# Gated linear attention and a dropless mixture of experts: attention by half chunks on 64x64 tiles, with another order of the steps

## The chip, the core and the metric

The kernel runs on one core of a Trainium2 chip. Such a core has a matrix engine (TensorE, written PE in the profile, with its weight loads as PEld), a vector engine (VectorE, DVE), a scalar engine (ScalarE, ACT), a general engine (GpSimd, POOL) and a queue that issues transfers (SyncE, SP). Matmul results go to PSUM[...]; everything else lives in SBUF or in DRAM. The metric is the time of one execution on the device in microseconds, and the median of several executions is compared.

## What is computed

Gated linear attention over 4 batches, 8 heads, 768 positions and a head size of 48, and then a mixture of 8 experts in which each of the 3072 tokens goes to its one best expert. All data are float32.

```python
# attention, per batch and head
for t in range(S):
    state = alpha[t][:, None] * state + outer(k[t], v[t])
    y[t] = q[t] @ state
x = y as (B*S, H*D) rows                      # 3072 x 384

logits = x @ w_gate                           # 8 experts
expert_idx = argmax(logits); gate_w = softmax(logits)[expert_idx]
for e in range(E):                            # its own tokens only
    y[e's rows] = relu(x[e's rows] @ w1[e]) @ w2[e]      # 384 -> 1024 -> 384
out = gate_w * y
```

## The kernel before

**Attention.** The sequence is cut into 24 chunks of 128 positions (`C`; six per batch, `NB`), and heads are taken in pairs (`NP` = 4), the two heads of a pair at partitions 0 and 64 (`DP` = 64). Within a chunk the product of the gates is turned into a running sum of logarithms. For chunk s the steps are:

- `load` (L186): alpha, k, q and v from DRAM by SP's queue, 192 KB each.
- `logs` (L197): ln of alpha on ScalarE.
- `cums` (L207): one matmul with a triangular matrix gives the running sums in the bank `cum`; ScalarE writes their exponentials `icp` (negative) and `cp`.
- `decay_out`, `decay_in` (L216, L220): the last row of `cp`, the decay over the whole chunk, is stored to DRAM and read back as a column `E` per head pair, both by ScalarE's queue.
- `operands` (L230): GpSimd multiplies k by `icp` and q by `cp`, into `kqb`.
- `transposes` (L236): eight transposes on TensorE; ScalarE copies `kT`, VectorE copies `qT`.
- `scores` (L248): k times q for each head, eight matmuls of 128 columns; the two heads of a pair stand in two row halves of the array and write two banks, `sA` and `sB`. VectorE masks one side into `dA`; ScalarE copies the other and GpSimd masks it into `dB`.
- `attend` (L266): into the bank `y` first the product of the state `U` of the chunk before with q ("inter", L274), then v times the masked scores (L280); then the chunk's own key-value product `kvp` (L291). VectorE copies `y` to `yT`, and the next state is (`kvp` + `U`) times `E`, with the sum on VectorE (`acc`) and the product on GpSimd.
- `rows` (L308): `yT` times a fixed matrix `back` (which holds the gate's weights too) gives token rows and negative logits in the bank `xr`; VectorE sums the logits into `lgn`.
- `keep_rows` (L317): ScalarE copies the rows to `xs`, and SP stores them to `x_rows` in DRAM.

**Routing**, by groups of one to four chunks: `choose` (L325) finds each token's expert on VectorE, `rank_products` (L346) counts tokens by two small matmuls into free columns of the bank `kvp`, `slots_of` (L353) turns the counts into slots, `one_hots` (L369) writes them as one-hot rows, and `tokens_of_slots` (L377) multiplies these into a table of tokens by slot.

**Order.** Each engine does its instructions in the order in which the program writes them. The loop (L409) runs s from -5 to 24. In one iteration TensorE gets `cums(s+4)`, `transposes(s+2)`, `rows(s-1)`, `scores(s+1)`, then inter, values and key-values of `attend(s)`. So each step reads what another engine prepared an iteration ago. Loads are issued 5 (v) to 8 iterations ahead. In the last iteration the remaining routing is done, and `indices` (L384) gives the token list of every expert block.

**Experts.** GpSimd gathers the tokens' rows by index (`gather`, L495), `turn` (L518) transposes them, `layer1` and `layer2` (L536, L547) are the two products, and the results are scattered to the output. The weights stand in three buffers; `fetch1` and `fetch2` load them.

Two instructions of different engines on the same PSUM tile are ordered by semaphores that the framework adds.

## Time and profile before

| | us |
|---|---|
| median of 3 executions | 488.6 (488.29 to 490.05) |
| the profiled execution, its time | 489.74 |
| the profiled execution, first to last instruction (span) | 488.0 |
| attention: start to the last value matmul | 158 |
| seam: from there to the first transpose of the expert stage (170.25) | 12 |
| expert stage: 170.25 to the end | 318 |

| in one attention iteration, mean of one | ns |
|---|---|
| product on GpSimd (128x384) | 996 |
| copy of 128x512 from PSUM, VectorE / ScalarE | 687 / 593 |
| matmul record, 48 rows, 128 columns moved | 285 |
| matmul record, key-value, 48 columns moved | 222 |
| weight load record, 128 / 64 columns | 187 / 138 |

The profile lists a float32 matmul as two records, so eight products are 16. The records of matmuls that run together overlap, and a record is longer than the distance from one start to the next; the distance is what counts. Times in the lists are from the start of the span. An arrow gives the instruction that ended an engine's wait. "x16" means that 16 like instructions are merged in one line.

In slices of 12.2 us the sixteen transfer engines are busy all the time up to 120 us, at 160 to 210 GB/s[...]; 16 transfers of expert weights of 1536 KB stand later. TensorE's granted clock is full except at the seam, where the mean is 0.50 from 164 to 170 us and 0.52 from 170 to 178 us.

### The profile page before, as it was taken

To read this page: it belongs to the slowest core of one execution; us is meant where nothing else is said; L and a number is where in the kernel's file an instruction comes from. 1 tells how busy PE (TensorE), PEld (TensorE's weight loads), DVE (VectorE), ACT (ScalarE), POOL (GpSimd) and SP (SyncE) were. 2 spreads that over 40 slices of the span, in tenths; PEclk is the share of its full clock that TensorE was granted. 3 is DMA by queue.
4 is the path that set the end of the run, shared out by engine and by line. 5 is a ranking of instruction groups with operands and counts; after the bars stand their busy time and mean duration, and the time that the engine had idled before them with its cause. 6 is when DMAs were issued, how large, how long until landed. Compare 5 with 4: busy or idle time off the path is not lost.

```text
span 488.0 us, 7370 instructions
## 1 busy us (share of the span) xinstructions
PE 457.6 (94%) x2881; PEld 297.4 (61%) x2881; DVE 142.3 (29%) x391; ACT 103.2 (21%) x209; POOL 137.8 (28%) x226
## 2 busy tenths in 40 slices
PE   2999999999999389999999999999999999999992
PEld 0788888888898275555555555555555455555451
DVE  2344766665778421212401201101201201301100
ACT  3544544544421001101001111011111001101010
POOL 3556745555642270010124010016020020010020
PEclk9999999999999779999999999999999999999997
DMA  9999999889992151300726400537300040000000
GB/s 161 199 177 203 207 210 203 168 170 272 299 356 107 50 160 39 142 32 8 267 75 211 135 32 0 189 118 249 129 28 16 1 166 22 1 20 16 2 32 25
DMA packets 127213, 59.76 MB, mean 122 GB/s; under 512 B 110304, under 2 KB 121604, under 8 KB 127178
## 3 DMA queue, kind: packets, MB, share of 16 engines
q1 hardware_dynamic: 114818, 48.87, 39.6%
q0 software_dynamic: 3584, 10.34, 6.4%
q10 hardware_dynamic: 8776, 0.08, 1.0%
q8 instruction: 23, 0.38, 0.3%
q14 instruction: 12, 0.10, 0.1%
HBM read 49.70 MB, written 10.35 MB: 123 GB/s over the span
## 4 chain that ended last, share of the span: by engine, by line
issue 54%; PE 27%; POOL 11%; DVE 2%; DMA 2%; SPq 1%; ACT 0%; POOLq 0%; ACTq 0%
POOL out_dram L559 6%; POOL xg L499 5%; PE sA L254 5%; PE y L280 4%; PE tp L241 4%; PE xr L313 4%; PE cum L210 4%; PE y L274 4%; PE kvp L291 2%; SPq L194 1%; DMA a_sb<-in_alpha_dram 1%; DMA x_rows<-xs 1%; DVE yT L295 1%; DVE sc L330 0%; DVE dA L258 0%
## 5 line engine op out<-in xcount | busy, mean ns | idle before, releaser
L528 PE MATMUL hp<-xT,w 128*128 128x448 f32 (+2 forms) x402 | 148.4, 530 | 1.2 <-DVE xT L524 1.2
L553 PE MATMUL zp<-w,h_sb 128*128 128x384 f32 (+1 forms) x512 | 146.8, 488 | 0.0
L528 PEld LDWEIGHTS hp<-xT,w 128*128 128x128 f32 x402 | 77.4, 194 | 69.9 <-issue 65.0
L553 PEld LDWEIGHTS zp<-w,h_sb 128*128 128x128 f32 (+1 forms) x512 | 81.1, 177 | 62.4 <-issue 13.6
L559 POOL DMA_INDIRECT out_dram<-zo,g_idx x28 | 27.7, 988 | 251.7 <-ACT zo L558 251.7
L542 DVE TENSOR_SCALAR h_sb<-hp 128x448 f32<-128x448 f32 x32 | 20.0, 624 | 218.4 <-PE hp L528 218.4
L544 ACT ACTIVATE h_sb<-hp 128x448 f32<-128x448 f32 x32 | 17.4, 543 | 142.0 <-PE hp L528 142.0
L558 ACT ACTIVATE zo<-zp,gw 128x384 f32<-128x384 f32 x28 | 16.3, 581 | 133.6 <-PE zp L553 129.0
L210 PE MATMUL cum<-ln,cmask 128*128 128x384 f32 x48 | 24.7, 601 | 8.7 <-ACT cp L214 4.4
L499 POOL DMA_INDIRECT xg<-x_rows,g_idx x28 | 26.9, 960 | 12.2 <-issue 12.2
L241 PEld LDWEIGHTS tp<-ident,kqb 128*128 128x128 f32 x192 | 23.5, 146 | 7.9 <-issue 4.2
L254 PE MATMUL sA<-qT,kT 48*128 48x128 f32 x192 | 27.7, 285 | 0.0
L254 PE MATMUL sB<-qT,kT 48*128 48x128 f32 x192 | 27.7, 285 | 0.0
L233 POOL TENSOR_TENSOR kqb<-k_sb,icp 128x384 f32<-128x384 f32 x24 | 23.9, 996 | 8.8 <-ACT icp L213 8.6
L241 PE MATMUL tp<-ident,kqb 128*128 128x128 f32 x192 | 26.2, 282 | 0.0
L280 PE MATMUL y<-dA,vb 128*64 128x128 f32 x192 | 26.1, 279 | 0.0
L280 PE MATMUL y<-dB,vb 128*64 128x128 f32 x192 | 26.1, 279 | 0.0
L313 PE MATMUL xr<-back,yT 128*128 128x104 f32 x192 | 25.4, 275 | 0.7 <-DVE yT L295 0.5
L261 POOL TENSOR_SCALAR_AFFINE_SELECT dB<-dB 128x512 f32<-128x512 f32 x24 | 15.2, 634 | 37.3 <-ACT dB L260 23.8
L254 PEld LDWEIGHTS sA<-qT,kT 48*128 48x128 f32 x192 | 23.1, 187 | 2.6 <-issue 0.3
L313 PEld LDWEIGHTS xr<-back,yT 128*128 128x128 f32 x192 | 23.3, 192 | 1.5 <-issue 1.0
L234 POOL TENSOR_TENSOR kqb<-q_sb,cp 128x384 f32<-128x384 f32 x24 | 23.9, 996 | 0.0
(117 smaller groups left out, 403.0 us busy)
## 6 DMA issues: line engine op xcount, KB each, us to landing
w<-in_moe_w_dram SPq DMA_DIRECT2D x16, 1536.0 KB, 6.8
x_rows<-xs SPq DMA_DIRECT2D x24, 196.0 KB, 2.9
a_sb<-in_alpha_dram SPq DMA_DIRECT2D x24, 192.0 KB, 4.1
k_sb<-in_k_dram SPq DMA_DIRECT2D x24, 192.0 KB, 3.8
q_sb<-in_q_dram SPq DMA_DIRECT2D x24, 192.0 KB, 4.0
vb<-in_v_dram SPq DMA_DIRECT2D x24, 192.0 KB, 4.6
Eb<-decay_rows ACTq DMA_DIRECT2D x40, 0.8 KB, 3.0
xg<-x_rows,g_idx POOLq DMA_INDIRECT x28, 3.1
```

Source lines behind the costliest of these rows:

```text
L210: nc.tensor.matmul(cum[:], lhsT=cmask[:], rhs=d["ln"][:], start=True, stop=True)
L233: nc.gpsimd.tensor_tensor(kq[:, 0, :, :D], d["k"][:], heads(d["icp"]), op=ALU.mult)
L234: nc.gpsimd.tensor_tensor(kq[:, 1, :, :D], d["q"][:], heads(d["cp"]), op=ALU.mult)
L241: nc.tensor.transpose(tp[:, p, :], pair(kqb[s % 4][:, i], p), ident[:])
L254: nc.tensor.matmul(t[:, p, :], lhsT=d["kT"][r : r + D, p, :], rhs=d["qT"][r : r + D, p, :], start=True, stop=True,)
L280: nc.tensor.matmul(y[r : r + DP, p, :], lhsT=d["v"][:, 2 * p + i, :], rhs=d["d" + "AB"[i]][:, p, :], start=(c == 0 and p == 0), stop=True, ...
L313: nc.tensor.matmul(xr[:, p, :], lhsT=d["yT"][:, p, :], rhs=back[:, p, :], start=True, stop=True)
L499: nc.gpsimd.indirect_dma_start(out=xg[:, j, :], out_offset=None, in_=x_d[:, :], in_offset=bass.IndirectOffsetOnAxis(ap=i, axis=0),)
L528: nc.tensor.matmul(hp[:, c0:c1], lhsT=w1[:, a, f * C : (f + 1) * C], rhs=xT[:, a, c0:c1], start=(a == 0), stop=(a == DB - 1), skip_group_c ...
L542: nc.vector.tensor_relu(h[:, f, :cols], hp[:, :cols])
L553: nc.tensor.matmul(zp[i * m : (i + 1) * m, :], lhsT=h[:, f, c0 : c0 + m], rhs=w2[:, f, :], start=(f == 0), stop=(f == FB - 1), skip_group_ ...
L559: ins = nc.gpsimd.indirect_dma_start(out=out[:, :], out_offset=bass.IndirectOffsetOnAxis(ap=idx, axis=0), in_=zo[:], in_offset=None, bound ...
```

## The change

The change is in attention alone, with the places where weights are fetched.

**Half chunks.** `HALVES` numbers four combinations of a half j of the chunk (64 positions) and a head a of the pair. Scores are computed only within a half: 64 keys by 64 queries. The state is kept twice: `U[:, 0]` before the first half and `U[:, 1]` before the second, which is `U[:, 0]` plus the key-value product of the first half. Each of inter, scores, values and key-values becomes 16 matmuls of 64 by 64 (48 rows where the head size is summed), four to a head pair, each in another quarter of the array. `at(j, a)` puts the output of head a of half j in the partitions that make this so. Rows take `yT` of both halves, as two column tiles, with a `back` for each half.

**PSUM.** One tile `y` of two banks, one per half, holds both the values (`y_ps`) and the key-values (`kv_ps`). One tile `scp` of two banks, one per head, holds the scores and four columns for the decays (`last_ps`). The sums' bank has spare columns in which `rank_products` now write.

**Decays.** The way through DRAM goes. A matmul with the last column of the identity takes the last row of `cp` out as a column, eight per chunk, and ScalarE copies them to `E`.

**Order.** s runs from -4 to 23, and an iteration gives TensorE: decays(s+2), key-values(s+1) and values(s); sums(s+3), ranks of the last group and transposes(s+2); inter(s+1) and scores(s+2); rows(s). VectorE: `state(s+1)` (both sums), `qT`, slots, one product with the mask for both heads (`dAB`), `lgn`, `choose`, one-hots. ScalarE: `E`, `results(s)` (the copy `yT`), `icp`, `cp`, `kT`, `xs`, ln. GpSimd: the decay of the state, then the operands.

**Loads** are listed in order of need (`loads`), three to four iterations ahead, with five buffers each for alpha, k and q. The store of a chunk's rows is issued at the start of the next iteration, ahead of that iteration's loads. Expert 0's weights are asked for in iteration 17 and expert 1's in iteration 20; before it was iteration 15, and expert 1's stood after attention in the program.

```diff
+    HALVES = [(j, a) for j in range(2) for a in range(2)]
+    def at(j, a):
+        return DP * (a ^ j)
...
-        def decay_out(s):
-            if s % NB + 1 < NB:
-                nc.scalar.dma_start(e_d[s : s + 1, :], st[s]["cp"][C - 1 : C, :])
-        def decay_in(s):
...
+        def decays(s):
+            for p in range(NP if s < NT else 1):
                 for a in range(2):
+                    h = (2 * p + a) * D
+                    nc.tensor.matmul(
+                        last_ps[half(a), p : p + 1], lhsT=cpb[s % 3][DP:, h : h + DP], rhs=ident[DP:, C - 1 :],
+                        start=True, stop=True, skip_group_check=True,
                     )
+            if s < NT and s % NB + 1 < NB:
+                st[s]["E"] = Eb[s % len(Eb)]
+                nc.scalar.copy(st[s]["E"][:], last_ps)
...
+        scp = ps.tile([C, 2, 512], F32, name="scp")
+        sc_ps = scp[:, :, : NP * DP].rearrange("r b (p t) -> r b p t", p=NP)
+        last_ps = scp[:, 1, NP * DP : NP * DP + NP]
+        y = ps.tile([C, 2, 512], F32, name="y")
+        y_ps = y[:, :, : NP * DP].rearrange("r b (p t) -> r b p t", p=NP)
+        kv_ps = y[:, :, NP * DP : NP * (DP + D)].rearrange("r b (p d) -> r b p d", p=NP)
+
+        def inter(s):
+            d = st[s]
+            for p in range(NP):
+                for j, a in HALVES:
+                    if j or s % NB:
+                        nc.tensor.matmul(
+                            y_ps[at(j, a) : at(j, a) + DP, j, p, :],
+                            lhsT=Ub[s % 2][head(a), j, p, :], rhs=d["qT"][head(a), p, half(j)],
+                            start=(p == 0), stop=False, skip_group_check=True,
+                        )
...
         def scores(s):
             for p in range(NP):
+                for j, a in HALVES:
                     nc.tensor.matmul(
+                        sc_ps[half(j), a, p, :], lhsT=d["kT"][head(a), p, half(j)], rhs=d["qT"][head(a), p, half(j)],
+                        start=True, stop=True, skip_group_check=True,
                     )
+            d["dAB"] = work.tile([C, 2, NP, DP], F32, name="dAB", bufs=3)
+            nc.vector.tensor_tensor(
+                d["dAB"][:], sc_ps, m64[:, None, None, :].to_broadcast([C, 2, NP, DP]), op=ALU.mult,
             )
 
         def attend(s):
+            n = s + 1
+            for p in range(NP):
+                for j, a in HALVES:
+                    if n < NT and (j == 0 or n % NB + 1 < NB):
+                        nc.tensor.matmul(
+                            kv_ps[half(a), j, p, :],
+                            lhsT=kqb[n % 4][half(j), 0, 2 * p + a, :], rhs=st[n]["v"][half(j), 2 * p + a, :D],
+                            start=(p == 0 and (s < 0 or (j == 0 and s % NB == 0))), stop=True, skip_group_check=True,
+                        )
...
+                    nc.tensor.matmul(
+                        y_ps[at(j, a) : at(j, a) + DP, j, p, :],
+                        lhsT=d["v"][half(j), 2 * p + a, :], rhs=d["dAB"][half(j), a, p, :],
+                        start=False, stop=True, skip_group_check=True,
+                    )
...
+        def state(s):
             c = s % NB
+            U = Ub[s % 2]
+            if c == 0:
+                nc.vector.tensor_copy(U[:, 1, :, :D], kv_ps[:, 0, :, :])
+            else:
+                nc.vector.tensor_tensor(U[:, 1, :, :D], kv_ps[:, 0, :, :], U[:, 0, :, :D], op=ALU.add)
             if c + 1 < NB:
+                acc = st[s]["acc"] = work.tile([C, NP, D], F32, name="acc")
+                nc.vector.tensor_tensor(acc[:], kv_ps[:, 1, :, :], U[:, 1, :, :D], op=ALU.add)
+
+        def results(s):
+            st[s]["yT"] = work.tile([C, 2, NP, DP], F32, name="yT")
+            nc.scalar.copy(st[s]["yT"][:], y_ps)
...
+        def loads(s):
+            for n, i in (("v", s + 1 + AHEAD), ("k", s + 2 + AHEAD), ("q", s + 2 + AHEAD), ("a", s + 3 + AHEAD)):
+                if 0 <= i < NT:
+                    load(n, i)
...
+        for s in range(-4, NT):
+            last = s == NT - 1
+            do(store_rows, s - 1)
+            loads(s)
+            if 0 <= s + 2 <= NT:
+                decays(s + 2)
+            if s + 1 >= 0:
+                attend(s)
+            do(state, s + 1)
+            if 0 <= s + 1 < NT and (s + 1) % NB + 1 < NB:
+                decay(s + 1)
+            do(results, s)
+            do(cums, s + 3)
             do(operands, s + 3)
+            ranked = []
+            for g in groups_of:
+                if g[-1] == s - 1:
+                    if last:
+                        sums_tile()
+                    ranked.append(rank_products(g, st["sums"][:, Dm : Dm + len(g) * E]))
             do(transposes, s + 2)
+            for r in ranked:
+                slots_of(*r)
+            do(inter, s + 1)
+            if s == NT - 2:
+                seen = work.tile([C, 2, 1], F32, name="seen")
+                nc.vector.tensor_copy(seen[:], y_ps[:, :, NP - 1, :1])
+            do(scores, s + 2)
+            if last:
                 while hots:
                     one_hots(hots.pop(0))
+                route = ps.tile([C, NP, C], F32, name="tp", bufs=2)[:].rearrange("r p t -> r (p t)")
+                tokens_of_slots(0, NT - 4)
+            do(rows, s)
+            do(keep_rows, s)
+            for g in groups_of:
+                if g[-1] == s:
+                    choose(g)
+            for _ in range(min(len(hots), 2 if len(hots) > 2 else 1)):
                 one_hots(hots.pop(0))
+            do(logs, s + 4)
+            late_consts(s + 2)
+            if s in (NT - 7, NT - 4):
+                e = (s - NT + 7) // 3
+                w_t[e] = fetch1(e), fetch2(e)
+        store_rows(NT - 1)
```

## The prediction

> **What bounds the kernel now.** I read the page first: what is busy, and when.

> ```profile
> span 488.0 us, 7370 instructions
> PE 457.6 (94%) x2881; PEld 297.4 (61%) x2881; DVE 142.3 (29%) x391; ACT 103.2 (21%) x209; POOL 137.8 (28%) x226
> ...
> PE   2999999999999389999999999999999999999992
> ...
> DMA  9999999889992151300726400537300040000000
> ```

> Each of the 40 slices is 12.2 us. TensorE is full except in the first slice and in slices 14 and 15, the seam between attention and the expert stage. The expert stage begins with the first transpose at 170.25 us (timeline) and keeps TensorE busy to the end; its work is not edited. So the question is when attention ends. Second, the timeline of one attention iteration on TensorE; columns are start and duration in us, then the instruction.

> ```profile
> 83.86 0.62 PE L291 MATMUL kvp<-vb,kqb 128*64 128x48 f32 x16
> ...
> 84.41 0.91 PE L210 MATMUL cum<-ln,cmask 128*128 128x384 f32 x2
> ...
> 85.16 1.04 PE L241 MATMUL tp<-ident,kqb 128*128 128x128 f32 x8
> ...
> 86.03 1.04 PE L313 MATMUL xr<-back,yT 128*128 128x104 f32 x8
> ...
> 88.09 1.09 PE L274 MATMUL y<-qT,Ub 48*64 48x128 f32 x16
> ```

> Each start is the end of the stage before. Sums 0.75, transposes 0.87, rows 0.97, scores 1.09 (87.00 to 88.09), inter 1.02 (to 89.11), weighted values 1.02 (to 90.13), key-value 0.55: 6.27, the chain of waits gives 6.16 after its rounding of ends. There is no hole: transposed tiles are used one iteration later, so no copy is waited for. Chunks that begin a batch lack inter; the mean from rows(0) (24.84) to inter(23), which follows rows(22) at 155.59, is 5.9.

> Third, the copies beside it:

> ```profile
> 84.68 0.35 DVE L301 TENSOR_TENSOR acc<-kvp,Ub 128x192 f32<-128x192 f32 x1
> ...
> 85.42 0.49 ACT L213 ACTIVATE icp<-cum 128x384 f32<-128x384 f32 x1 [0.58 <-PE cum L210]
> ...
> 85.81 0.49 ACT L214 ACTIVATE cp<-cum 128x384 f32<-128x384 f32 x1
> ...
> 86.18 0.59 ACT L246 COPY kT<-tp 128x512 f32<-128x512 f32 x1
> ```

> Read the steps between starts: 0.39 and 0.37, so ScalarE takes 1.35 from the start of icp to the end of kT. Fourth, a wait in the tail that decides much below:

> ```profile
> 158.62 1.12 PE L313 MATMUL xr<-back,yT 128*128 128x104 f32 x8
> ...
> 161.12 0.18 DVE L315 TENSOR_REDUCE lgn<-xr 128x8 f32<-128x32 f32 x1
> ...
> 161.47 0.48 ACT L320 COPY xs<-xr 128x384 f32<-128x384 f32 x1 [4.44 <-DVE lgn L315]
> ```

> ScalarE was idle for 4.44 us, the rows were done at 159.74, yet it waited for a VectorE read of other columns of the same PSUM tile. Accesses of two engines to one PSUM tile are kept apart, reads too.

> [...]scores to inter, the next start comes 0.21 after the last instead of 0.11 and the second 0.16 after that, 0.15 in all. [...](y from dA and dB load 6 to 7 ns apart and run together); no run here shows four tiles.[...]

> **The change part by part.**

> 1. TensorE's own work. With 64 columns of weights, a key-value pair takes (0.62 - 0.222) / 7 = 0.057: eight pairs take 0.62 with the last one's tail. A quad of four 64x64 tiles streams 64 or 48 columns; I take one quad pass as one such pair, 0.058. Bounds: 0.055 and 0.116 (two pairs in turn). Key-value, values, inter and scores are 8 quad passes each: 4 x 0.47. The new decays are 16 loads with one column on one row half: 8 pairs, 0.47. Rows on two column tiles: 104 columns against the old bound of 128 weight columns; the first old rows pass, its weights ready, took 0.09; 8 x 0.09 = 0.73. Sums 0.75 and transposes 0.87 stay. Sum 4.70; four mode changes at 0.15 add 0.6 (the old order had about as much): 5.3, against 6.2. If this were all, 0.9 x 22 iterations = 20 us would go.

> 2. The new order makes TensorE wait. Time 0 is the first decay matmul; decays, key-value and values end at 1.41, the last one's tail at 1.63. state (VectorE) reads the key-value columns of the two banks that the values are written to; by the bank wait it starts after both: U 1.68 to 2.03, acc 2.06 to 2.41 (0.35 each). results (ScalarE) reads the same banks: from 2.58 (0.17 handover, as 161.30 to 161.47) to 3.17. Behind it in ScalarE's order stand icp 3.07, cp 3.46, kT 3.83 to 4.42. And scores now need kT of their own iteration: 4.57 (0.15 handover, as ScalarE's ln to the first sums, 4.15 to 4.30). TensorE could have been there at 3.8: transposes end at 3.13, and only inter (0.47, with its mode change) lies between. Scores to 5.05, rows to 6.0, next decays at 6.15. dA's product (0.69) ends at 6.02 and lets the decays, which share a scores bank, start at 6.17. So an iteration takes about 6.15: the 0.9 saved is waited away.

> 3. rank_products now write the sums' bank and stand between sums and transposes. By the bank wait they start after cp: 4.1 to 4.3 in such an iteration (choose, 1.64 on VectorE in 147.03 to 148.67, delays state by 0.3), so transposes start at 4.35, not 2.26. kT and qT then follow, scores at 6.3, not 4.57, and the period is about 8.0: +1.85 each. In-loop groups with sums: after chunks 3, 7, 11, 15 and 18, so 5 x 1.85 = 9.2 us. Bounds 0 (no wait) and 12 us. In the old order the ranks went to the key-value bank, and no reader stood before them.

> 4. Decays without DRAM: 40 loads and 20 stores leave ScalarE's queue (1.0% of 16 engines x 488 = 4.9 us of DMA time). Not on the path: 4.8 us of DMA per chunk (alpha loads issued from 39.76 to 78.19: 8 chunks) hides under an iteration of either length. The select on POOL (0.63) and the copies dB and dA of one side go; they were no bound. The new copy of E (128x4, ScalarE) falls ahead of results, while ScalarE waits anyway. Cost 0.

> 5. Loads in order of need. Iteration 0 now needs the 12th load, alpha of chunk 3, instead of the 14th. The 12th was issued at 11.20 and lands some 4 us later; logs 0.52: 15.8 at the earliest. The sums at 4.30 took 1.62 where 0.91 is normal[...] and the pipeline is a chain of short waits, so I take 17.5 for the start of iteration 0 and 23.6 for the end of rows(0), against 25.7 (24.84 + 0.87). Gain 2, bounds 0 and 4.

> 6. Stores move ahead of the loads in SP's order, and wait for xs(s-1), so five loads stand behind each such wait; they have three iterations of lead, 18 us against 4. Cost 0; if the lead went, 1 us an iteration. Expert 1's weights are now asked for in iteration 20, and hidden until after 170 us. Both 0. So are the tiles that move from one pool to another, the copy to `seen` and the lone decay pair of chunk 24: each is one short instruction where its engine is free.

> 7. Tail. After rows(22), rank(22) waits for choose(22), then 20 token matmuls (16 took 1.52, so 0.085 apart), then rows(23): 2.3 + 0.1 + 1.7 + 0.9 and 0.3 to lgn(23), 5.3. Before: 155.59 to 161.12, 5.5. The rest is the same. 0, bounds -1 and +2 (the clock's slow stretch of 13.7 us there may shift).

> Sum: rows(0) to rows(22). After: 19 iterations at 6.11 (the batch's last chunk saves 0.24) = 116.1, ranks 9.2, then 6.1, 6.1 and 4.6 for iterations 20 to 22, which lose sums, transposes and scores in turn but wait for choose: 142.1. Before: 155.6 - 25.7 = 129.9. So +12.2, less 2 from the start: +10.2. The profiled execution took 489.74 (span 488.0 and 1.7 around it): 499.9. The median is 488.6: 498.8, rounded to 499.

> **The rivals.**

> A. The case above: the chain through VectorE and ScalarE sets the period, and ranks wait. 499; with the period 0.3 shorter or longer, 492 to 506.

> B. On the other side, faster: state starts after its own key-value matmuls, results do not wait for it, ranks do not wait for cp. Then qT is the last: transposes end 3.29, copy to 4.02, scores 4.17, period 5.7: 19 x 5.66 + 5.7 + 5.7 + 4.5 = 123.4, against 129.9: -6.5 - 2 = 480. It decides if the bank wait is not applied between disjoint columns here; the row reduction and xs speak against it.

> C. The chain holds but ranks do not stall: 499 - 9 = 490.

> D. Four tiles do not run together: pairs, so +0.47 for key-value, values and scores: 1.41 x 21 = 30: 529. For it: only diagonal pairs are seen. Against: column pairs and row pairs each run at full overlap.

> E. Issue-bound quads: eight instructions in 58 ns at the 6.5 ns seen within pairs leave no room; 0.073 a quad gives about 0.48 x 21 = 10: 509.

> **How the numbers follow.** A 0.50, B 0.19, C 0.13, D 0.10, E 0.08. A is the likeliest: 499. 481 to 512 leaves out D and about half of B. What can be told from no change is 0.5%, 2.4 us: 486.2 to 491.0. Slower: A, D, E and little of C, 0.69. Same: most of C and edges, 0.13. Faster: B, 0.18. A's own range is 492 to 506.

> **What would show it.** Step 1: 16 or 32 matmuls a group and quads 0.058 apart in the timeline. Step 2: results released by DVE acc, and scores' weight loads idle some 0.7 us released by ACT kT; a period of 6.1 between sums. Step 3: rank matmuls released by ACT cp, five iterations near 8. Step 5: rows(0) ending near 23.6. I am wrong if TensorE shows no hole ahead of scores, or if rows(22) ends before 155.

## The result, and the profile after

| | before | after |
|---|---|---|
| median, us | 488.5 | 509.0 |
| executions, us | 488.29 to 490.05 | 505.18 to 509.41 |
| ratio, 95% interval | | 1.039 (1.032 to 1.045) |
| the profiled execution: time / span, us | 489.74 / 488.0 | 505.18 / 503.3 |
| end of rows(0), us | 25.7 | 26.9 |
| end of rows(22), us | 155.6 | 172.4 |
| first transpose of the expert stage, us | 170.25 | 185.46 |
| from there to the end, us | 317.8 | 317.9 |

The kernel is 20 us slower by the medians, 15.3 by the two profiled spans. The expert stage is as long as before, so all of the 15.3 lies before it. Medians, here and below, are over all executions of a version; one that was disturbed (516.33 in after) is left out of the range and of the ratio. The profiled execution was the fastest: two others took 508.5 and 509.4, with a mean granted clock of 0.960, where the profiled one had 0.966.

The page of after first; the rows with digits are 40 slices of 12.6 us.

```profile
span 503.3 us, 11568 instructions
PE 453.3 (90%) x4997; PEld 288.3 (57%) x4997; DVE 128.7 (26%) x396; ACT 104.3 (21%) x229; POOL 127.0 (25%) x206
...
PE   4898988888878839999999999999999999999992
...
PEclk9899999999899578999999999999999999999997
...
q8 instruction: 40, 0.66, 0.6%
```

And two rows of the page of before that were not shown:

```profile
PEclk9999999999999779999999999999999999999997
...
q8 instruction: 23, 0.38, 0.3%
```

TensorE's row in attention was all nines and is eights now: it is busy for 4 us less in all and yet the span is longer, so it waits. Two more things differ. The granted clock dips within attention (slices 2, 11 and 14), not only at the seam. And queue 8, which brings pieces of the program itself, moved 40 packets of 16 KB where it was 23. TensorE's instructions, matmuls and weight loads together, are 9994 against 5762.

The timeline of one iteration of after, with the columns start, duration, instruction; what stands in brackets is the idle time before it and what ended that:

```profile
93.22 0.91 PE L225 MATMUL cum<-ln,cmask 128*128 128x384 f32 x2
...
93.80 0.36 DVE L344 TENSOR_TENSOR acc<-y,Ub 128x192 f32<-128x192 f32 x1
...
94.27 0.59 ACT L348 COPY yT<-y 128x512 f32<-128x512 f32 x1 [1.25 <-DVE acc L344]
...
94.75 0.50 ACT L228 ACTIVATE icp<-cum 128x384 f32<-128x384 f32 x1
...
95.14 0.50 ACT L229 ACTIVATE cpb<-cum 128x384 f32<-128x384 f32 x1
...
95.50 0.61 ACT L267 COPY kT<-tp 128x512 f32<-128x512 f32 x1
96.16 0.56 PEld L298 LDWEIGHTS scp<-qT,kT 48*64 48x64 f32 x32 [0.69 <-ACT kT L267]
96.17 0.69 PE L298 MATMUL scp<-qT,kT 48*64 48x64 f32 x32 [0.55 <-ACT kT L267]
...
96.79 0.93 PE L356 MATMUL xr<-back,yT 128*64 128x104 f32 x16
...
99.29 0.91 PE L225 MATMUL cum<-ln,cmask 128*128 128x384 f32 x2
101.79 0.19 PE L397 MATMUL cum<-ohs,ones_sq 128*128 128x32 f16 x1 [1.59 <-ACT cpb L229]
```

This is the chain of step 2. VectorE's `acc` ends at 94.16, ScalarE's copy of the results follows at 94.27, then `icp`, `cp` and `kT` one behind the other, and scores start when `kT` is done; TensorE's weight loads were idle for 0.69 us. From sums to sums it is 6.07. The last line is the next iteration, in which the ranks wait 1.59 for `cp`: step 3.

What no step had is in the timeline of TensorE alone, in after:

```profile
40.12 0.23 PE L323 MATMUL y<-dAB,vb 64*64 64x64 f32 x1
41.12 0.68 PE L323 MATMUL y<-dAB,vb 64*64 64x64 f32 x27 [0.77 <-issue]
41.73 0.91 PE L225 MATMUL cum<-ln,cmask 128*128 128x384 f32 x2
...
163.22 0.34 PE L298 MATMUL scp<-qT,kT 48*64 48x64 f32 x7
164.63 0.58 PE L298 MATMUL scp<-qT,kT 48*64 48x64 f32 x25 [1.07 <-issue]
165.14 1.37 PE L356 MATMUL xr<-back,yT 128*64 128x104 f32 x16
```

(The two parts are from two stretches of that timeline.) TensorE stops for about a microsecond in the middle of a group of like matmuls, whose operands are all there, and the profile names nothing that it waited for. I call that a hole, and count each step of more than 0.42 us between two starts on TensorE that no wait explains, less the usual 0.06 (the two records of the sums always start 0.43 apart; there a hole counts when it adds more than 0.42 to that). After has six in attention, 5.1 us in all (at 36.4, 40.1, 80.3, 124.7, 143.2 and 163.3); before has none. In the records of queue 8, each of the six ends 1.3 to 1.6 us after a 16 KB piece of program has landed.

The holes also stand at fixed places of the program. Count all instructions of TensorE in the trace, control instructions too: 1217, 1473, 3521, 5825, 6593 and 7617 of them come before the ends of the six holes. Each of these numbers is 193 more than a multiple of 256. It is so for all 80 holes of all the runs here, and each of the 80 ends 1.2 to 1.7 us after a landing. So a hole is a wait at the edge of a piece of 256 instructions: TensorE has used up the piece it has, and the next one has only just landed.

In the last line of the view rows need 1.37 us where 0.93 is normal: from 165.48 on the granted clock is 0.5, for 10.24 us.

### The profile page after: what moved, and what is told of

The parts are those of the page before. It is cut to its first block, busy times and chain, and to the rows that moved or that the text cites. A ratio compares the mean times of both kernels' runs of the same rounds, so it can differ in the third digit from the quotient of the medians.

```text
span 503.3 us, 11568 instructions
## 1 busy us (share of the span) xinstructions
PE 453.3 (90%) x4997; PEld 288.3 (57%) x4997; DVE 128.7 (26%) x396; ACT 104.3 (21%) x229; POOL 127.0 (25%) x206
## 4 chain that ended last, share of the span: by engine, by line
issue 55%; PE 20%; POOL 9%; DVE 6%; ACT 5%; DMA 2%; SPq 0%; POOLq 0%; ACTq 0%; DVEq 0%
POOL out_dram L628 5%; PE xr L356 4%; PE scp L298 3%; POOL xg L568 3%; PE tp L262 2%; PE y L313 2%; PE y L323 2%; ACT icp L228 2%; PE scp L243 1%; ACT cpb L229 1%; ACT kT L267 1%; PE cum L225 1%; PE hp L597 1%; DVE Ub L341 1%; DMA a_sb<-in_alpha_dram 1%
## 5 line engine op out<-in xcount | busy, mean ns | idle before, releaser
L568 POOL DMA_INDIRECT xg<-x_rows,g_idx x28 | 26.9, 960 | 11.2 <-issue 7.9
L262 PEld LDWEIGHTS tp<-ident,kqb 128*128 128x128 f32 x192 | 24.3, 151 | 7.0 <-issue 4.7
L262 PE MATMUL tp<-ident,kqb 128*128 128x128 f32 x192 | 27.8, 292 | 0.0
L298 PE MATMUL scp<-qT,kT 48*64 48x64 f32 x768 | 17.6, 227 | 11.0 <-ACT kT L267 7.2
L265 DVE COPY qT<-tp 128x512 f32<-128x512 f32 x24 | 16.6, 691 | 34.9 <-PE tp L262 34.9
L255 POOL TENSOR_TENSOR kqb<-q_sb,cpb 128x384 f32<-128x384 f32 x24 | 24.0, 998 | 0.0
L356 PE MATMUL xr<-back,yT 128*64 128x104 f32 x384 | 23.7, 268 | 0.0
L366 ACT COPY xs<-xr 128x384 f32<-128x384 f32 x24 | 11.5, 478 | 58.0 <-DVE lgn L361 49.9
L323 PE MATMUL y<-dAB,vb 64*64 64x64 f32 x768 | 21.3, 230 | 2.3 <-issue 2.3
L303 DVE TENSOR_TENSOR dAB<-scp,m 128x512 f32<-128x512 f32 x24 | 16.6, 691 | 24.5 <-PE scp L298 24.1
L298 PEld LDWEIGHTS scp<-qT,kT 48*64 48x64 f32 x768 | 14.3, 137 | 14.2 <-ACT kT L267 9.5
L593 DVE COPY xT<-xtp 128x384 f32<-128x384 f32 (+1 forms) x32 | 14.8, 503 | 26.7 <-PE xtp L591 26.7
```

The source lines that it names most:

```text
L255: nc.gpsimd.tensor_tensor(kq[:, 1, :, :D], d["q"][:], heads(d["cp"]), op=ALU.mult)
L262: nc.tensor.transpose(tp[:, p, :], pair(kqb[s % 4][:, i], p), ident[:])
L298: nc.tensor.matmul(sc_ps[half(j), a, p, :], lhsT=d["kT"][head(a), p, half(j)], rhs=d["qT"][head(a), p, half(j)], start=True, stop=True, sk ...
L323: nc.tensor.matmul(y_ps[at(j, a) : at(j, a) + DP, j, p, :], lhsT=d["v"][half(j), 2 * p + a, :], rhs=d["dAB"][half(j), a, p, :], start=Fals ...
L356: nc.tensor.matmul(xr[half(j), p, :], lhsT=d["yT"][:, j, p, :], rhs=back[:, j, p, :], start=True, stop=True, skip_group_check=True,)
L568: nc.gpsimd.indirect_dma_start(out=xg[:, j, :], out_offset=None, in_=x_d[:, :], in_offset=bass.IndirectOffsetOnAxis(ap=i, axis=0),)
```

## The experiments

All are edits of after, but the last. Ratios are to the kernel before, run on the same chip (488.9 in the first group of four, 490.7 in the second, 490.6 in the third), so versions of different groups are compared by their ratios. The base period is the distance of two sums in an iteration with neither ranks nor a hole; half clock is the time between 18.7 us and the expert stage in which the granted clock was 0.5. Both and the holes are from the profiled execution.

| run | median | ratio (95%) | base period | holes: number, us | half clock |
|---|---|---|---|---|---|
| after | 509.0 | 1.039 (1.032 to 1.045) | 6.1 | 6, 5.1 | 16.6 |
| e1 results first | 520.3 | 1.063 (1.060 to 1.066) | 5.7 | 12, 20.2 | 36.6 |
| e2 ranks late | 501.8 | 1.021 (1.018 to 1.025) | 6.1 | 6, 6.4 | 20.5 |
| e3 scores with slack | 498.4 | 1.022 (1.017 to 1.028) | 5.4 | 6, 5.4 | 24.4 |
| e4 decays by DRAM | 512.8 | 1.045 (1.042 to 1.048) | uneven | 5, 3.7 | 24.3 |
| e5 ranks late and slack | 495.6 | 1.010 (1.006 to 1.014) | 5.4 | 14, 12.2 | 17.2 |
| e6 no inter | 515.0 | 1.046 (1.042 to 1.051) | 6.1 | 4, 4.7 | 32.9 |
| e7 old load order | 514.0 | 1.045 (1.041 to 1.049) | 6.1 | 5, 4.9 | 17.5 |
| e8 e5, decays by SP | 525.3 | 1.070 (1.066 to 1.073) | uneven | 3, 2.2 | 46.9 |
| e9 short filler | 519.8 | 1.059 (1.057 to 1.061) | 6.1 | 10, 9.8 | 31.0 |
| e10 long filler | 512.8 | 1.044 (1.037 to 1.051) | 6.1 | 6, 6.7 | 21.6 |
| e11 e5, wide decays | 498.9 | 1.012 (1.004 to 1.019) | 5.9 | 3, 3.0 | 15.8 |
| e12 before, store first | 490.5 | 1.000 (0.999 to 1.001) | 6.2 | 0, 0.0 | 4.6 |

Executions of one version of after lie up to 1.5% apart, so a difference of 3 us between two versions settles nothing. Holes and half clock are those of one traced execution each.

**e1: the results' copy ahead of the state.** It takes one link out of the chain.

```diff
+            do(results, s)
             do(state, s + 1)
...
-            do(results, s)
```

> Edit of the changed kernel: the copy of the results (ScalarE) is written ahead of the state's two sums (VectorE), which read the same two PSUM banks. Chain theory (VectorE sums, then the copy, icp, cp, kT, one behind the other because of the bank wait, set the period of 6.05 us): the copy starts 0.8 us earlier, kT ends about 0.4 earlier, qT is then last at 4.17 us from the first decay matmul instead of 4.5, so the period falls to 5.75 and the time by about 7 us, to 502. Rival (TensorE's own pace with four small tiles sets the period): no change, 509 within 2.

The chain was right: where nothing disturbed it the period fell from 6.07 to 5.70. But the whole got 11 us slower (ratio 1.063 against 1.039), with four times the time in holes and twice the half clock. The bank wait also stands the other way round now (timeline of e1):

```profile
64.69 0.59 ACT L348 COPY yT<-y 128x512 f32<-128x512 f32 x1 [2.02 <-PE y L323]
65.38 0.36 DVE L341 TENSOR_TENSOR Ub<-y,Ub 128x192 f32<-128x192 f32 x1 [3.43 <-ACT yT L348]
```

VectorE reads the key-value columns 0.1 us after ScalarE has read the value columns: two readers of one tile keep apart, whichever comes first. A faster chain alone gained nothing here, since holes and half clock grew.

**e2: ranks behind scores.**

```diff
-                    ranked.append(rank_products(g, st["sums"][:, Dm : Dm + len(g) * E]))
             do(transposes, s + 2)
-            for r in ranked:
-                slots_of(*r)
...
             do(scores, s + 2)
+                    ranked.append(rank_products(g, st["sums"][:, Dm : Dm + len(g) * E]))
+            for r in ranked:
+                slots_of(*r)
```

> Edit of the changed kernel: rank_products and slots_of stand after the scores instead of between sums and transposes. Rank theory (they wait for cp, which reads the same bank): five iterations of about 7.5 us become 6.1, so 7 us less, 502. Rival (those iterations are long because VectorE is busy with choose and slots): no change or 1 us less.

Four of the five rank iterations now take 6.2 to 6.3 us once the holes in two of them are taken off, against 7.1 to 8.2 in after; the fifth lies at half clock. The base period stayed at 6.1. Measured by the ratios (1.039 and 1.021), 8 us went. That agrees with the 8.1 us that the rank iterations of after take over its base period (step 3 below).

**e3: scores one iteration later.** `kT` then has a whole iteration.

```diff
-            do(scores, s + 2)
+            do(scores, s + 1)
```

> Edit of the changed kernel: an iteration computes scores(s+1) instead of scores(s+2), so kT and qT were copied an iteration ago, as in the kernel before. Chain theory: no wait ahead of scores, the period falls from 6.05 to TensorE's own 5.3 to 5.4, about 14 us less, 495; the ranks' waits stay. Rival (TensorE's own pace): no change. If instruction supply is a limit of its own, the gain is smaller, 5 to 9 us, with holes inside groups of like matmuls.

The base period fell to 5.4, so the wait for `kT` is worth 0.7 an iteration; the rank iterations at full clock still took 7.3. The start gained too: rows(0) end 2.6 us earlier, near the 23.6 of the prediction. Against that stand 7.8 us more of half clock, which at half speed is an estimated 3.9 us of work lost.

**e5: both.**

```diff
-                    ranked.append(rank_products(g, st["sums"][:, Dm : Dm + len(g) * E]))
...
-            do(scores, s + 2)
+            do(scores, s + 1)
+                    ranked.append(rank_products(g, st["sums"][:, Dm : Dm + len(g) * E]))
```

> Both edits of the changed kernel together: ranks after the scores, and scores(s+1) in place of scores(s+2). Chain theory alone: both waits go, 5.4 us an iteration throughout, 485. With the limit on TensorE's instruction supply (holes of 0.5 to 2 us, each ending 1.3 to 1.6 us after a 16 KB piece of its program has landed, 5 us in all in the changed kernel) more iterations meet it the faster they go: 490 to 498.

From e5's timeline:

```profile
69.06 0.69 PE L288 MATMUL y<-qT,Ub 48*64 48x64 f32 x32
...
69.57 0.65 PE L298 MATMUL scp<-qT,kT 48*64 48x64 f32 x32
69.66 0.60 ACT L267 COPY kT<-tp 128x512 f32<-128x512 f32 x1
...
70.15 0.19 PE L397 MATMUL cum<-ohs,ones_sq 128*128 128x32 f16 x1
```

Scores start before this iteration's `kT` is copied, and neither they nor the ranks wait. It has the lowest median of the versions with the change in it (e11's interval overlaps its own), and is still 1% slower than before. The holes more than doubled, to 14 and 12.2 us. The two waits were worth some 21 us (0.7 in each of 19 iterations, and 8); 7 of these came back as holes. TensorE now wants its 340 instructions every 5.4 us and not every 6.1.

**e6: no inter.** This leaves out the product of state and query, so the output lacks what earlier halves add. The values' first matmul then starts the sum in `y`, as inter's did.

```diff
-                        start=False, stop=True, skip_group_check=True,
+                        start=(p == 0), stop=True, skip_group_check=True,
...
-            do(inter, s + 1)
```

> Edit of the changed kernel that leaves out the product of the state with q (inter), so the output lacks what earlier positions add; 64 of TensorE's 340 instructions an iteration go, all of them from the place where it waits for kT anyway. Chain theory: the usual period stays 6.05 us. Supply theory: the holes inside groups go, 5 us, and the half-clock stretches of attention with them, 2 to 5 us: 500. Rival (TensorE's own pace): 0.6 us an iteration, 13 us less, with a period of 5.45.

From the lists of waits between 30 and 150 us (total, number of times, longest), after:

```profile
PEld scp L298 <- ACT kT L267: 8.1, 13, 0.7
```

and e6:

```profile
PEld scp L298 <- ACT kT L267: 19.2, 15, 1.4
```

Half a microsecond of work less on TensorE, and the period is still 6.1: what went was waited instead. So the chain sets the pace, and not TensorE. The time of 500 that I had expected was wrong: in the traced execution the clock was halved for 32.9 us, twice as long as in after.

**e7: the old order of loads.** Loads of alpha, k, q eight chunks ahead and v four, in the old grouping.

```diff
-            for n, i in (("v", s + 1 + AHEAD), ("k", s + 2 + AHEAD), ("q", s + 2 + AHEAD), ("a", s + 3 + AHEAD)):
+            for n, i in (("a", s + 8), ("k", s + 8), ("q", s + 8), ("v", s + 4)):
```

> Edit of the changed kernel: loads in the order of before (alpha, k and q of four chunks ahead of the first v, then those eight iterations ahead), buffers 5, 6 and 6. If the order of need gains at the start as predicted, rows(0) ends 2 us later than in the changed kernel (28.9 against 26.9) and the time is 2 us more. Rival (the start is set by the chain of waits at half clock, not by loads): no difference in rows(0) beyond 0.5 us.

The last rows(0) matmul starts at 34.1, not 26.6. In the new pipeline the order of need is worth 7.5 us at the start. In the whole, by the ratios (1.045 and 1.039), some 3 us of them show, and the two intervals overlap.

**e4 and e8: decays through DRAM again**, on ScalarE's queue with the order of after (e4), or on SP's queue with the order of e5 (e8); one pair of decay products stays in both.

```diff
-            for p in range(NP if s < NT else 1):
+            for p in range(1):
...
-                nc.scalar.copy(st[s]["E"][:], last_ps)
...
+            do(decay_out, s + 3)
+            do(decay_in, s + 2)
```

> Edit of the changed kernel: decays go through DRAM again as before; of the decay matmuls one pair per chunk is kept, its result unused. Chain theory: decays stand at the head of the chain, so 0.37 us of each iteration goes, about 8 us less, 501, less what ScalarE's three transfer issues (about 1 us an iteration) give back. Rival (decays lie beside other work): no change, or 2 us more from the issues.

> The two edits of e5 and the decays through DRAM on SP's queue, stored at the end of an iteration and read back at the start of the next; one decay pair per chunk stays, unused. TensorE loses 0.37 us and 28 instructions an iteration: by its own pace 5.0 us, so 8 us less than e5, more if fewer instructions also mean fewer holes. Rival (E comes too late from DRAM, and the state waits for it, as in e4): no gain over e5, and GpSimd's decay of the state is released by a transfer.

From the waits of e4:

```profile
PE cum L226 <- ACT ln L215: 15.5, 14, 2.4
...
ACT ln L215 <- DMA Eb<-decay_rows: 6.0, 4, 1.8
```

and of e8:

```profile
POOL Ub L340 <- DMA Eb<-decay_rows: 41.6, 9, 6.2
...
ACT xs L376 <- DMA x_rows<-xs: 21.1, 7, 3.6
```

e8 is clearly slower than e5; e4 shows no gain over after (their intervals overlap). In e4 three issues of transfers on ScalarE delay ln, and the sums wait for it; in e8 the decays arrive late behind SP's loads. The short pipeline has no room for the way through DRAM on either queue: here it gains nothing on the 0.47 us of TensorE that the products take in an iteration. These two have fewer instructions, and fewer holes.

**e9 and e10: filler in the wait for kT.** TensorE has about 0.6 us there with nothing to do. e9 puts 8 short matmuls in (32 instructions, like the decays), e10 two long ones (8 instructions); what they write is not read.

```diff
+                for p in range(NP):
+                    for a in range(2):
+                        h = (2 * p + a) * D
+                        nc.tensor.matmul(
+                            scp[half(a), 1, 400 + p : 401 + p], lhsT=cpb[(s + 2) % 3][DP:, h : h + DP],
+                            rhs=ident[DP:, C - 1 :], start=True, stop=True, skip_group_check=True,
+                        )
             do(scores, s + 2)
```

and for e10

```diff
+                for _ in range(2):
+                    nc.tensor.matmul(
+                        scp[:, 1, 400:], lhsT=ident[:], rhs=ident[:, :112], start=True, stop=True, skip_group_check=True,
+                    )
             do(scores, s + 2)
```

> After with 8 more decay-like matmuls (32 records, some 0.47 us of TensorE) in each iteration, just ahead of scores, where TensorE waits 0.7 us for kT; what they write is read by nothing. Supply theory (TensorE's instructions come in pieces and can't follow a faster pace): about a tenth more instructions in the same period, so more than the 6 holes and 5.1 us of after, 8 to 12 us of holes, base period still 6.1, and a time of 511 to 518. Rival (the holes come from other traffic and not from how many instructions are wanted): holes as in after, and 509 give or take 3, or less if a busier TensorE keeps its clock.

> After with 2 long matmuls (8 records of 112 columns, some 0.4 us of TensorE) in the same place, so the same busy time as the short filler with a quarter of its instructions. Supply theory: holes as in after (5 to 6 us), base period 6.1, and 507 to 511. If the clock falls because TensorE stands idle, less half clock than the 16.6 us of after, and down to 503.

From e9's timeline of TensorE:

```profile
95.73 0.69 PE L288 MATMUL y<-qT,Ub 48*64 48x64 f32 x32
96.26 0.59 PE L493 MATMUL scp<-ident,cpb 64*64 64x1 f32 x16
96.68 0.69 PE L298 MATMUL scp<-qT,kT 48*64 48x64 f32 x32
...
99.22 0.30 PE L323 MATMUL y<-dAB,vb 64*64 64x64 f32 x4
100.58 0.58 PE L323 MATMUL y<-dAB,vb 64*64 64x64 f32 x24 [1.07 <-issue]
```

and from e10's:

```profile
63.83 0.70 PE L491 MATMUL scp<-ident 128*128 128x112 f32 x4
64.45 0.69 PE L298 MATMUL scp<-qT,kT 48*64 48x64 f32 x32
```

The fillers take 0.42 us from start to start in e9 and 0.62 in e10, and both leave the base period at 6.1. With the long ones there are as many holes as in after (6, 6.7 us); the short ones, with a tenth more instructions, made 10 and 9.8 us of them and a time 7 us above e10's, with intervals that don't touch. Of all the runs this shows best that the holes go with the number of instructions. That a busier TensorE keeps its clock did not come true in e9 (mean granted clock 0.943 to 0.958, after 0.960 to 0.966). e10 settles nothing there: more half clock before the expert stage, but a mean clock over its executions of 0.958 to 0.974.

**e11: e5 with decays of 128 columns**, four matmuls for eight.

```diff
-                        last_ps[half(a), p : p + 1], lhsT=cpb[s % 3][DP:, h : h + DP], rhs=ident[DP:, C - 1 :],
+                    last_ps[:, p : p + 1], lhsT=pair(cpb[s % 3], p)[DP:], rhs=ident[DP:, C - 1 :],
```

> Ranks behind scores and scores of the next chunk, as in the kernel at 495.6, and the decays by 4 matmuls of 128 columns in place of 8 of 64: 16 of some 340 instructions an iteration less. Supply theory: holes of about 11 us in place of 12.2, period 5.3, and 493 to 496. Rival (holes don't go with the number of instructions, and the path is set by VectorE and ScalarE): 495.6 give or take 1.

From e11's timeline:

```profile
64.00 0.96 PEld L241 LDWEIGHTS scp<-ident,cpb 64*128 64x128 f32 x8 [0.28 <-issue]
...
64.98 0.56 PEld L311 LDWEIGHTS y<-vb,kqb 64*64 64x64 f32 x32
```

I had missed that 128 columns load one after the other where two tiles of 64 load side by side: 0.98 us for 0.47, so the period is 5.9 and not 5.3. The holes shrank from 12.2 to 3.0 us, and the time did not move by more than the scatter: what was saved in holes was given up in the period. As a test of the supply alone this edit is poor, since it changed the pace too.

**e12: before, with the rows' store ahead of the loads.**

```diff
+            do(store_rows, s - 2)
             do(load, s + 8 if s + 8 >= 4 else -1, "akq")
...
-            nc.sync.dma_start(x_d[s * C : (s + 1) * C, :], xs[:])
```

> The kernel before with one part of the change alone: the store of a chunk's rows goes ahead of the iteration's loads in SP's order (one iteration later than its rows are ready). In the kernel before, ScalarE waited 3.7 us for such a store near 39 us. If stores behind loads cost time there, 2 to 4 us go: 485 to 487. If that wait is hidden, as step 6 has it, 488.6 give or take 1.

No difference, to a thousandth. ScalarE's wait for that store is hidden in the kernel before.

No version beat the kernel before.

## Why the prediction was right, and how much it missed

The direction, the likeliest case and its mechanism held; the size was +20 by the medians where I had +10, and 509 lies in the range of 481 to 512 but outside the likeliest case's own 492 to 506. That 509 fell inside the wide range is in part luck: half of the 20 comes from terms that the sum did not have. Rival E's 509 is a coincidence: its cause, quads bound by issue within the array, is not there. A limit on instructions there is, but in their supply.

**Step 1, right.** Scores start at 96.17 and the 32nd of their records 0.48 later: 0.06 a quad pass, where 0.058 was put in. Rows took 0.73, as said. So rivals D and E fall, and the doubt about four tiles at once is settled for this case: they do run together.

**Step 2, right.** Scores start 4.50 after the first decay (4.57), the weight loads idle 0.69 (0.7), the period is 6.07 (6.15), and `yT` waits for `acc`. e3 and e6 confirm it from both sides; rival B falls.

**Step 3, right, slightly large.** The five rank iterations took 7.05, 8.69 (1.03 of it a hole), 7.55, 8.20 (partly at half clock) and 7.94. Over 6.07 that is 8.1 us, against 9.2. e2 gave back 8; rival C falls.

**Step 4, cost 0: not contradicted.** The decays' 0.47 us was in step 1's sum; and with the way through DRAM in their place the time is no less (e4, e8).

**Step 5 failed in its size.** I had rows(0) at 23.6; they ended at 26.9, 1.2 later than before instead of 2 earlier. I let iteration 0 begin at 17.5, when its loads are there; it began at 20.85. The two iterations before it took 7.0 and 6.8 us (first decays at 7.13, 14.09 and 20.85), since they already wait for copies (0.88 us for `qT`, then 0.87 twice for `dAB`) and run in part at half clock (0.5 from 15.30 to 18.71). In e3 rows(0) ended at 24.3, within 0.7 of where I had them. The order of need does gain, 7.5 us by e7, but the new pipeline would have been that much later without it.

**Step 6, cost 0: right** for the store's place, as far as e12 shows it in the kernel before. Its other parts were not tried alone.

**Step 7 and the last iterations.** rows(22) to the expert stage: 13.1 us against 14.7, so -1.6 where step 7 had 0 and a lower bound of -1: 0.6 outside it. The sum's last three iterations took 19.3 us, not 16.8: a hole of 1.2, and from 165.48 on the half clock (rows(22) needed 1.71 us for 0.95).

**What the sum lacked: holes and clock.** Against the spans' +15.3 the sum of +10.2 is short by 5.1: the start 3.2; rows(0) to rows(19) 0.9, which is five holes of 3.9 less 1.1 for the ranks and 1.9 for a period of 6.0; the last three iterations 2.5; the seam -1.6. The other 5 of the 20 lie between the profiled execution and the medians (508.96 - 505.18 = 3.8 for after, 1.2 for before), and no trace shows them; the slower executions have the lower mean clock, which fits.

The diff had the sign of it: four small matmuls stand for one or two large ones in each of several steps, about 340 instructions in an iteration for 164, and I priced them by their time in the array alone. By the traces a piece of 16 KB holds 256 of them: the holes stand multiples of 256 apart, and 9994 / 256 = 39 pieces came in 40 packets on queue 8, 5762 / 256 = 22.5 in 23. In the expert stage of after a piece starts to move when TensorE has 285 to 301 instructions left before it, so about one piece ahead. A piece lasts 256 / 340 of an iteration, 4.6 us at 6.1 and 4.1 at 5.4.

What is shown: a hole is a wait for the next piece; in no run was a piece in use less than 1.2 us after its landing, and in before each had at least 5.2 us; holes grow with instructions (9.8 us in e9 against 6.7 in e10) and with pace (12.2 us in e5 against 5.1 in after and 3.0 in e11). The traces also show where a piece is late: it starts to move late. In after's attention, from 18 us on, a median of 164 instructions is left at that moment, and 17 at the worst, while the transfer itself takes 0.9 to 1.7 us (0.9 to 1.3 in the expert stage). The sixteen transfer engines are 74 to 96% busy there (by stretches of about 20 us from 18 to 160) and 24% in the expert stage, so the piece may stand behind other transfers. That reason is argued and not shown, since no experiment took the traffic away. The rule is not strict either: e3 at 5.4 had only 5.4 us, at the same number of instructions as e5.

The clock stays partly open. Its stretches come after gaps (below), so that holes and waits cost more than their length. But e6 had fewer holes than after and more half clock, so I can't tell its share for a single run beforehand.

## What to carry to other kernels

When work is cut into more and smaller matmuls, count the engine's instructions against the time in which they must arrive, not only the time in the array: here 55 a microsecond left holes, and 27 did not. A pipeline shortened by one iteration turns copies on other engines into waits (0.69 us for `kT` here); follow the chain in the order of each engine, with every reader of a shared PSUM tile in it. And a wait taken off the path pays less than its length when the engine behind it is close to its next limit: e5 removed two waits, got a third of their worth back as holes, and stayed 1% behind the kernel before.
